# GpSimd's queue issues 112 weight transfers that SP's queue issued: the second MoE's output weights, and its combined input weights

## The chip, the cores and the metric

The kernel runs on one core of one Trainium2 chip. The time is that of one launch in device microseconds; where several runs of a kernel are shown, the median counts. The engines are TensorE (PE in the profile, its weight loads PEld), VectorE (DVE), ScalarE (ACT), GpSimd (POOL) and SyncE (SP, which here does nothing but issue DMAs).

## The reference, cut to what matters

```python
# attention: 4 batches, 8 heads, 576 positions, head_dim 64
q_rot, k_rot = rotate(q), rotate(k)                  # rotary embedding
scores = np.matmul(q_rot, k_rot.transpose(0, 1, 3, 2)) / np.sqrt(64)
attn = softmax(scores)
x = np.matmul(attn, v)                               # -> [2304, 512]
# first MoE: 512 -> 768 -> 512
h = np.maximum(np.maximum(x @ w1, x @ w2), x @ w3)
x = h @ moe_w_out
# second MoE: 512 -> 2048 -> 512
h = x @ moe2_w_in
g = h * (1.0 / (1.0 + np.exp(-h)))
out = g @ moe2_w_out
```

Some weights come as words of 8 bytes; the kernel makes fp32 values of them ("narrows" them) on the chip.

## The kernel before

**Stages.** One fused kernel. From the start to about 545 us it runs attention, tile by tile (a tile is up to 128 query positions of two heads), and between the tiles the first MoE for the batches whose attention is finished; beside both, the weights are prepared. Up to about 620 us the first MoE's last batch follows, and from there on the second MoE. Products of fp32 values are made from high and low fp16 halves, and the second MoE's two layers use seven products in place of eight (as in Strassen's method), for which sums of weight blocks are needed.

**Attention around the change.** For each pair of heads q and k are loaded (`load_qk`, L305 and L308), rotated on GpSimd (`rope_steps`: L366, L367 and L370 for three pieces of the tile, nine steps in all) and transposed on TensorE (`qk_turn`, L387). For each tile TensorE makes the scores (L433 to L443), VectorE their maximum (`tile_max`, L453), ScalarE the exponentials (L460) and their normalisation (`tile_norm`, L472); four DMAs from SP's queue move them between partitions (`tile_move`, L511, pt<-e), VectorE turns blocks of 32x32 in place (`tile_flip`, L533), and TensorE multiplies by v (L578).

**Narrowing.** `narrow_w2` runs 32 pieces of 128x256 for w_in ("wi") and then 32 for w_out ("wo"). A piece is loaded (L858, z64, 256 KB, four buffers), ScalarE takes its high half into z (L229, four buffers), VectorE adds the low half (L241, L248, L249), ScalarE measures it (L155), and the narrowed piece is stored in DRAM: L833 for wi (zwi), L838 for wo (zwo). A z buffer comes round again four pieces later.

**Combined items.** When wi is narrowed and its scale is known, `prep_w8` makes 16 items. Item k loads four blocks from zwi (L965, za, 256 KB, two buffers); GpSimd makes four sums of them (L971, zs, two buffers); ScalarE casts the blocks to fp16 high halves (L948) and VectorE makes the low halves (L952), in w8o (three buffers), for the four loaded blocks and for the four sums; each half is stored in DRAM (L979, w8scr, 256 KB). The second MoE reads w8scr (`w8_load`, L1376 and L1379) and zwo (`prep_w7`, L1001) from about 545 us on.

**What sets the order.** The engines run in order, each its own list. The lists come from a scheduler that simulates the program as it is written (`TileContext` with `schedule_with_timeline_sim=True`), within data dependences, the rings of buffers, and marks (`tc.issue_after`) that keep an instruction behind another one. The load L858 stands behind such a mark: `last["load"]`, the latest load of q and k. All DMAs are issued by SP, but for a few by ScalarE at the start.

Of the kernel before, what the change touches and what calls it, by code (L numbers as in the profile page):

```python
# [22 lines left out]
def fused_kernel(  # L23
# [22 lines left out]
    nc = tc.nc  # L46
# [62 lines left out]
    w8scr = dram.tile([P, NF2 // 2, 2, 2, 8, P], F16, name="w8scr")  # L109
    zscr = {nm: dram.tile([P, KC * (F2 // 512) * 512], F32, name="z" + nm) for nm in ("wi", "wo")}  # L110
# [56 lines left out]
    def flat(t):  # L167
        return t.rearrange("p a b -> p (a b)")
# [112 lines left out]
    last = {}  # L281
# [538 lines left out]
    def narrow_w2(W, src, nm):  # L820

        part = {}
        M = W.m * 512 // 256
        for n in range(M + 5):
            if n >= 5:
                W.measure(n - 5)
                if nm == "wi":
                    i, o = divmod(n - 5, 2)  # L830
                    q, c = divmod(i, KC)
                    half, f = divmod(4 * q + 2 * o, HB)
                    nc.sync.dma_start(  # L833
                        out=zscr[nm].rearrange("p (f c a i n) -> p f c a i n", c=2, a=2, i=2, n=P)[:, f:f + 2, c % 2, c // 2, half],
                        in_=W.t[n - 5].rearrange("p (f n) -> p f n", n=P),
                    )
                else:
                    nc.sync.dma_start(out=zscr[nm][:, (n - 5) * 256:(n - 4) * 256], in_=W.t[n - 5])  # L838
            if 3 <= n <= M + 2:
                with tc.issue_after(last["max"]):  # L840
                    W.narrow_low(part.get(n - 3))
                    W.narrow_b(n - 3, part.pop(n - 3, None))
            if 2 <= n <= M + 1:
                if wide:
                    W.t[n - 2] = z_p.tile([P, 256], F32, tag="z", name="z")
                with tc.issue_after(exps[-1]):
                    W.narrow_a(n - 2, part.get(n - 2), low=False)
            if n < M:
                i, o = divmod(n * 256, 512)
                if nm == "wi":  # L850
                    q, c = divmod(i, KC)
                    from_ = src[c * P:(c + 1) * P, q * 512 + o:q * 512 + o + 256]
                else:
                    from_ = src[i * P:(i + 1) * P, o:o + 256]
                if wide:
                    part[n] = z64_p.tile([P, 256], w1.dtype, tag="z64", name="z64")
                    with tc.issue_after(last["load"]):
                        nc.sync.dma_start(out=part[n], in_=from_)  # L858
                else:
                    W.t[n] = z_p.tile([P, 256], F32, tag="z", name="z")  # L860
                    nc.sync.dma_start(out=W.t[n], in_=from_)
            yield
        t = W.scale_a(n=M)
        yield
        with tc.issue_after(last["score"]):
            W.scale_b("s" + nm, t)
        yield
# [59 lines left out]
    def timed(steps):  # L927

        n = 0
        for t, fn in sorted(steps, key=lambda x: x[0]):  # L930
            while n < t:
                n += 1
                yield
            fn()

    def half_of(W, nm):

        x = const.tile([P, 1], F32, name=nm + "half")
        nc.vector.tensor_scalar(out=x, in0=W.s, scalar1=0.5, scalar2=None, op0=ALU.mult)
        return x  # L940
# [5 lines left out]
    def cast_high(h, x, s, behind):  # L946
        with tc.issue_after(behind):
            nc.scalar.activation(out=h, in_=x, func=AF.Copy, scale=s)  # L948

    def cast_low(l, h, x, s, behind):  # L950
        with tc.issue_after(behind):
            nc.vector.scalar_tensor_tensor(out=l, in0=x, scalar=s, in1=h, op0=ALU.mult, op1=ALU.subtract)  # L952

    def prep_w8(step):

        sw = half_of(WI, "wi")
        steps = []

        def item(k):
            f, c = divmod(k, 2)  # L960
            z, w = {}, {}

            def load():
                z[0] = za_p.tile([P, 4, P], F32, tag="za", name="za")
                nc.sync.dma_start(out=flat(z[0]), in_=zscr["wi"][:, (2 * f + c) * 512:(2 * f + c + 1) * 512])  # L965

            def sums():
                z[4] = zs_p.tile([P, 4, P], F32, tag="zs", name="zs")
                block = lambda i: z[i // 4 * 4][:, i % 4]
                for o, x, y, op in SUMS:  # L970
                    nc.gpsimd.tensor_tensor(out=block(o), in0=block(x), in1=block(y), op=op)  # L971

            def high(a):
                w[a] = w8o_p[0].tile([P, 2, 4, P], F16, tag="w8o", name="w8o")
                cast_high(flat(w[a][:, 0]), flat(z[a]), sw, exps[-1])

            def low(a):
                cast_low(flat(w[a][:, 1]), flat(w[a][:, 0]), flat(z[a]), sw, last["max"])
                nc.sync.dma_start(out=w8scr[:, f, c, :, a:a + 4], in_=w[a])  # L979

            t = k * step
            for d, fn in ((0, load), (2, sums), (2.1, lambda: high(0)), (2.9, lambda: low(0)), (3, lambda: high(4)), (3.9, lambda: low(4))):
                steps.append((t + d, fn))

        for k in range(2 * HB):
            item(k)
        yield from timed(steps)
# [338 lines left out]
    def narrow_all():  # L1326
        yield from narrow_w2(WI, wi2, "wi")
        yield from narrow_w2(WO, wo2, "wo")
# [117 lines left out]
```

## Time and profile before

| | |
|---|---|
| median of 3 runs | 968.02 us (966.81 to 968.2) |
| the profiled execution, its own time | 970.68 us |
| its span | 969.0 us |
| TensorE's mean granted clock | 0.983 |
| TensorE busy | 901.6 us (93%) |
| VectorE busy | 709.6 us (73%) |
| ScalarE busy | 609.4 us (63%) |
| GpSimd busy | 441.1 us (46%) |

The span is the time from the first to the last instruction in the profiled execution; its own time has some 1.7 us around it. Busy shares are means over stages that differ: where an engine is not the one that ends the waits of a stage, its idle time costs nothing. The chain of waits is followed from the last instruction back, at each step to what released it.

### The profile page before, as it was taken

How to read it: one execution, taken by the hardware profiler on the slowest of the kernel's cores; microseconds unless marked ns; L12 is line 12 of the kernel's file. 1: busy time of each engine (PE TensorE's matmuls, PEld its weight loads, DVE VectorE, ACT ScalarE, POOL GpSimd, SP SyncE). 2: the span in 40 equal slices, each digit the busy share in tenths (PEclk: the TensorE clock that was granted, in tenths of full speed). 3: DMA queues.
4: the chain of work that ended last, by engine and by line, in shares of the span. 5: the costliest groups of instructions: out<-in, count | busy, mean ns of one | idle time of the engine just before them, and what ended most of it. 6: DMA issues, size and time to landing. Idle time of an engine off the chain costs nothing.

```text
span 969.0 us, 19018 instructions
## 1 busy us (share of the span) xinstructions
PE 901.6 (93%) x6802; PEld 669.0 (69%) x6802; DVE 709.6 (73%) x1271; ACT 609.4 (63%) x1405; POOL 441.1 (46%) x482
## 2 busy tenths in 40 slices
PE   3887998999999999989998999999998999999997
PEld 1443665666665666656654687788887888888886
DVE  6779888877788676898887677465786766856654
ACT  1987677757788777789877534363654545545442
POOL 6745485870325502321211047264486467464363
PEclk9799998999999999999999999999999999999999
DMA  6953035858888985899999763273543434424101
GB/s 154 285 146 108 14 100 126 186 110 179 200 172 196 221 159 135 218 241 228 263 223 204 183 206 110 63 230 113 157 158 99 136 122 136 127 87 137 61 1 44
DMA packets 178798, 146.29 MB, mean 151 GB/s; under 512 B 50960, under 2 KB 160272, under 8 KB 178704
## 3 DMA queue, kind: packets, MB, share of 16 engines
q1 hardware_dynamic: 177200, 144.36, 58.0%
q8 instruction: 54, 0.88, 0.4%
q10 hardware_dynamic: 1504, 0.72, 0.3%
q14 instruction: 40, 0.33, 0.1%
HBM read 90.51 MB, written 26.21 MB: 120 GB/s over the span
## 4 chain that ended last, share of the span: by engine, by line
PE 54%; DMA 8%; DVE 8%; ACT 5%; POOL 4%; issue 3%; SPq 3%; DVEq 0%; ACTq 0%; POOLq 0%
PE m L673 12%; PE m L1103 7%; DMA pt<-e 5%; PE mb L1103 5%; PE c L1166 4%; PE b L1166 4%; PE a L1166 3%; PE xp L578 3%; PE s L443 3%; PE mg L673 3%; POOL gsum L1050 2%; PE d L1166 2%; SPq L511 2%; DVE pt L533 1%; DVE nb L453 1%
## 5 line engine op out<-in xcount | busy, mean ns | idle before, releaser
L673 PEld LDWEIGHTS <-w 128*128 128x128 f16 x1632 | 159.1, 98 | 61.0 <-issue 17.8
L673 PE MATMUL m<-x,w 128*128 128x256 f16 (+1 forms) x1356 | 186.9, 286 | 10.6 <-DVE t L692 5.4
L1166 PEld LDWEIGHTS <-g 128*128 128x128 f16 x1485 | 145.8, 98 | 17.2
L1103 PEld LDWEIGHTS <-w8s 128*128 128x128 f16 x1344 | 131.2, 98 | 16.3 <-issue 1.0
L453 DVE TENSOR_REDUCE nb<-s 128x2 f32<-128x1152 f32 (+1 forms) x80 | 98.6, 1233 | 40.7 <-PE s L443 34.1
L460 ACT ACTIVATE e<-s,nb 128x576 f32<-128x576 f32 x144 | 105.3, 736 | 29.8 <-DVE nb L453 27.2
L472 ACT ACTIVATE e<-e,rec 128x576 f32<-128x576 f32 x144 | 104.1, 767 | 9.3 <-DVE rec L470 8.9
L366 POOL TENSOR_TENSOR w<-qk,sin_sb 128x512 f32<-128x512 f32 (+2 forms) x40 | 43.4, 1087 | 128.1 <-DMA qk<-in_q_dram 122.5
L443 PE MATMUL s<-T 64*128 64x512 f32 x256 | 80.7, 701 | 0.0
L578 PE MATMUL xp<-pt,vd 128*64 128x256 f32 (+1 forms) x512 | 76.5, 414 | 0.2 <-DVE pt L533 0.2
L533 DVE STREAM_TRANSPOSE pt<-pt 128x1024 f32<-128x1024 f32 (+1 forms) x60 | 67.7, 1129 | 11.9 <-DMA pt<-e 11.6
L971 POOL TENSOR_TENSOR zs<-za 128x128 f32<-128x128 f32 x32 | 17.1, 554 | 119.9 <-DVE w8o L952 46.1
L1117 POOL TENSOR_TENSOR z<-t 128x256 f32<-128x256 f32 x32 | 27.1, 847 | 89.0 <-DVE t L1109 53.9
L1055 DVE SCALAR_TENSOR_TENSOR g<-gsum,sg,g 128x1024 f16<-128x1024 f32 x36 | 49.2, 1372 | 24.5 <-ACT g L1054 24.1
L1054 ACT ACTIVATE g<-gsum,sg 128x1024 f16<-128x1024 f32 x36 | 40.9, 1143 | 37.8 <-POOL gsum L1050 37.8
L673 PE MATMUL m<-h,wo 128*128 128x256 f16 (+1 forms) x448 | 61.7, 286 | 0.0
L673 PEld LDWEIGHTS <-wo 128*128 128x128 f16 x512 | 49.7, 98 | 14.7 <-issue 2.0
L578 PEld LDWEIGHTS xp<-pt,vd 128*64 128x64 f32 x512 | 35.1, 136 | 34.4 <-issue 12.3
L944 POOL TENSOR_TENSOR z<-z 128x256 f32<-128x256 f32 x32 | 30.1, 964 | 42.1 <-DMA z<-zwo 41.6
L1166 PE MATMUL b<-w,g 128*128 128x256 f16 x376 | 48.5, 273 | 0.0
L1166 PE MATMUL c<-w,g 128*128 128x256 f16 x376 | 48.1, 274 | 0.0
L1166 PE MATMUL a<-w,g 128*128 128x256 f16 x376 | 47.9, 273 | 0.0
(266 smaller groups left out, 1998.1 us busy)
## 6 DMA issues: line engine op xcount, KB each, us to landing
w8s<-w8scr SPq DMA_DIRECT2D x64, 448.0 KB, 4.3
pt<-e SPq DMA_DIRECT2D x192, 128.0 KB, 4.1
z<-in_moe_w_in_dram SPq DMA_DIRECT2D x32, 256.0 KB, 3.6
z<-in_moe_w_out_dram SPq DMA_DIRECT2D x32, 256.0 KB, 3.9
w8scr<-w8o SPq DMA_DIRECT2D x32, 256.0 KB, 3.6
w<-in_moe_w_dram SPq DMA_DIRECT2D x6, 768.0 KB, 5.0
wo<-in_moe_w_dram SPq DMA_DIRECT2D x6, 768.0 KB, 5.4
qk<-in_q_dram SPq DMA_DIRECT2D x32, 128.0 KB, 3.6
```

The lines of the kernel that those rows point to most:

```text
L366: tt(out=w4, in0=t4, in1=sin2, op=ALU.mult)
L443: last["s"] = last["score"] = nc.tensor.matmul(s[:, o:o + 512], qs[r], kt[r], start=True, stop=True).ins
L453: x = nc.vector.tensor_reduce(out=nb[:, 0:m], in_=both(s, 0, 960, 576) if m > 1 else s[:, 0:576], op=ALU.max, axis=AX.X, negate=True)
L460: x = nc.scalar.activation(out=e[:, HK[g]], in_=s[:, SK[g]], func=AF.Exp, bias=nb[:, g:g + 1], accum_out=sm[:, g:g + 1])
L472: nc.scalar.activation(out=e[:, HK[g]], in_=e[:, HK[g]], func=AF.Copy, scale=r[:, g:g + 1])
L533: nc.vector.transpose(out=x, in_=x)
L578: nc.tensor.matmul(xp[r, 0:n], v4[:, g, c, :], turned(c, g), start=False, stop=(c == 3))
L673: x = nc.tensor.matmul(ps[:, 0:n], l, r, start=(first and i == 0), stop=(not more and i == len(passes) - 1))
L1054: nc.scalar.activation(out=h, in_=x, func=AF.Copy, scale=sg_t[jb])
L1055: nc.vector.scalar_tensor_tensor(out=l, in0=x, scalar=sg_t[jb], in1=h, op0=ALU.mult, op1=ALU.subtract)
L1103: nc.tensor.matmul(o, l, r, start=(i == 0), stop=(i == len(passes) - 1))
L1166: x = nc.tensor.matmul(ps, l, r, start=first, stop=last_, skip_group_check=True)
```

## The change

Four groups of DMAs go from SP's queue (`nc.sync`) to GpSimd's (`nc.gpsimd`): the stores of narrowed pieces of w_out (L838, 32), the loads of w_out's pieces (L858, only where `nm` is "wo", 32), the loads of the items (L965, 16) and the stores of the items' halves (L979, 32). w_out's loads also lose the mark that keeps them behind the latest load of q and k. The loads and stores of w_in's pieces stay on SP, as do all transfers of attention. What is computed, the buffers and their numbers stay the same.

```diff
--- before.py
+++ after.py
@@ -835,7 +835,7 @@
                         in_=W.t[n - 5].rearrange("p (f n) -> p f n", n=P),
                     )
                 else:
-                    nc.sync.dma_start(out=zscr[nm][:, (n - 5) * 256:(n - 4) * 256], in_=W.t[n - 5])
+                    nc.gpsimd.dma_start(out=zscr[nm][:, (n - 5) * 256:(n - 4) * 256], in_=W.t[n - 5])
             if 3 <= n <= M + 2:
                 with tc.issue_after(last["max"]):
                     W.narrow_low(part.get(n - 3))
@@ -854,8 +854,8 @@
                     from_ = src[i * P:(i + 1) * P, o:o + 256]
                 if wide:
                     part[n] = z64_p.tile([P, 256], w1.dtype, tag="z64", name="z64")
-                    with tc.issue_after(last["load"]):
-                        nc.sync.dma_start(out=part[n], in_=from_)
+                    with tc.issue_after(last["load"]) if nm == "wi" else nullcontext():
+                        (nc.sync if nm == "wi" else nc.gpsimd).dma_start(out=part[n], in_=from_)
                 else:
                     W.t[n] = z_p.tile([P, 256], F32, tag="z", name="z")
                     nc.sync.dma_start(out=W.t[n], in_=from_)
@@ -962,7 +962,7 @@
 
             def load():
                 z[0] = za_p.tile([P, 4, P], F32, tag="za", name="za")
-                nc.sync.dma_start(out=flat(z[0]), in_=zscr["wi"][:, (2 * f + c) * 512:(2 * f + c + 1) * 512])
+                nc.gpsimd.dma_start(out=flat(z[0]), in_=zscr["wi"][:, (2 * f + c) * 512:(2 * f + c + 1) * 512])
 
             def sums():
                 z[4] = zs_p.tile([P, 4, P], F32, tag="zs", name="zs")
@@ -976,7 +976,7 @@
 
             def low(a):
                 cast_low(flat(w[a][:, 1]), flat(w[a][:, 0]), flat(z[a]), sw, last["max"])
-                nc.sync.dma_start(out=w8scr[:, f, c, :, a:a + 4], in_=w[a])
+                nc.gpsimd.dma_start(out=w8scr[:, f, c, :, a:a + 4], in_=w[a])
 
             t = k * step
             for d, fn in ((0, load), (2, sums), (2.1, lambda: high(0)), (2.9, lambda: low(0)), (3, lambda: high(4)), (3.9, lambda: low(4))):
```

The lists of the other engines hardly change. On GpSimd, the list has 503 rows in place of 391. The place below lies in the last rope (qk_4464 is the tile of q and k that it turns, w_4816 its scratch, cos_sb and sin_sb the tables), at about 390 us in the trace of before; names with a number are tiles, the number telling one buffer's use from the next.

```order
+L971 TENSOR_TENSOR zs_4679<-zs_4679,za_4489 128x128
+L979 DMA w8scr_136<-w8o_4496 128x2x512
+L965 DMA za_4677<-zwi_137 128x512
+L858 DMA z_3_4675<-in_moe_w_out_dram 128x256
+L838 DMA zwo_138<-z_4485 128x256
 L366 TENSOR_TENSOR w_4816<-qk_4464,sin_sb_120 128x128
+L971 TENSOR_TENSOR zs_4679<-za_4489,zs_4679 128x128
+L979 DMA w8scr_136<-w8o_4581 128x2x512
+L971 TENSOR_TENSOR zs_4847<-za_4677 128x128 x2
+L858 DMA z_0_4723<-in_moe_w_out_dram 128x256
+L838 DMA zwo_138<-z_4575 128x256
```

The rope's step L366 is the only row that stands there in both lists: around it now stand issues of all four groups, and the sums L971 of the items in za_4489 and za_4677, which all stood behind the rope's last step before. In the same way the first two items' loads L965 and sums now stand before and between the steps of an earlier rope (qk_3941, the third from the end).

On SP, the same stretch of the list:

```order
-L858 DMA z_0_4477<-in_moe_w_out_dram 128x256
-L838 DMA zwo_138<-z_4330 128x256
-L979 DMA w8scr_136<-w8o_4417 128x2x512
-L965 DMA za_4489<-zwi_137 128x512
 L717 DMA yscr_135<-t_4602 128x320
 L511 DMA pt_4454<-e_4380 32x8x128 x4
```

The load and the store of a piece, the store of an item's half and the load of an item are gone from the place ahead of the first MoE's store (L717) and of the four DMAs of a tile of attention (L511), which stay in their order.

## Rows read from the trace of the kernel before

**Rows 1.** the page: part 4, shares of the chain; part 5, one group.

```profile
PE 54%; DMA 8%; DVE 8%; ACT 5%; POOL 4%; issue 3%; SPq 3%; DVEq 0%; ACTq 0%; POOLq 0%
L1117 POOL TENSOR_TENSOR z<-t 128x256 f32<-128x256 f32 x32 | 27.1, 847 | 89.0 <-DVE t L1109 53.9
```

**Rows 2.** busy time by engine, 392 to 545 us, columns named first.

```profile
core 0: us, PE busy (x) PEld busy (x) DVE busy (x) ACT busy (x) POOL busy (x), PEclk, DMA share, GB/s
392.00:545.00 153.00, 142.78 (x952) 90.10 (x951) 127.54 (x257) 128.11 (x354) 28.52 (x57) 1.00 0.95 228
```

**Rows 3.** the chain of waits in 392 to 545 us, its shares by line.

```profile
by line: DMA pt<-e 24.7%; PE m L673 11.5%; issue 8.5%; SPq L511 7.3%; ACT e L472 4.8%; DVE nb L453 4.4%; PE xp L578 4.0%; PE s L443 3.5%; DVE pt L533 3.4%; DMA z<-in_moe_w_out_dram 3.0%; ACT e L460 2.8%; ACT junk L155 2.8%; DVE z L249 2.4%;
```

**Rows 4.** the waits in 392 to 545 us: us in total, times, longest.

```profile
DVE pt L533 <- DMA pt<-e: 9.1, 4, 3.5
```

**Rows 5.** SP issues by line, 380 to 560 us: ns min/median/max, first and last.

```profile
L858 SPq DMA_DIRECT2D z<-in_moe_w_out_dram x28: 332/411/1043, 382.6 to 520.7; - x28
L838 SPq DMA_DIRECT2D zwo<-z x32: 319/432/748, 383.0 to 543.4; - x32
DMA to landing us min/median/max: 1.7/3.8/5.5
L965 SPq DMA_DIRECT2D za<-zwi x14: 320/404/483, 384.0 to 525.7; - x14
L979 SPq DMA_DIRECT2D w8scr<-w8o x32: 370/434/1826, 383.6 to 545.0; - x32
```

**Rows 6.** timeline of ScalarE and SP: start us, us, engine, line, operation.

```profile
405.25 1.43 ACT L472 ACTIVATE e<-e,rec 128x576 f32<-128x576 f32 x2
443.96 1.43 ACT L472 ACTIVATE e<-e,rec 128x576 f32<-128x576 f32 x2
406.55 0.75 SPq L838 DMA_DIRECT2D zwo<-z  x1
407.39 2.67 SPq L511 DMA_DIRECT2D pt<-e  x4
445.42 2.64 SPq L511 DMA_DIRECT2D pt<-e  x4
```

**Rows 7.** DMA issues in 392 to 545 us: KB each, median us to landing.

```profile
w8scr<-w8o SPq DMA_DIRECT2D x30, 256.0 KB, 3.7
z<-in_moe_w_out_dram SPq DMA_DIRECT2D x27, 256.0 KB, 3.9
zwo<-z SPq DMA_DIRECT2D x31, 128.0 KB, 3.8
za<-zwi SPq DMA_DIRECT2D x13, 256.0 KB, 4.0
```

**Rows 8.** timeline of GpSimd and VectorE at 304 us.

```profile
304.10 1.44 POOL L370 TENSOR_TENSOR qk<-qk,w 128x512 f32<-128x512 f32 x1
304.36 1.33 DVE L248 TENSOR_SCALAR z<-z 128x256 int32<-128x256 int32 x1
```

**Rows 9.** VectorE groups, 392 to 545 us: busy us, mean ns, idle before.

```profile
L248 DVE TENSOR_SCALAR z<-z 128x256 int32<-128x256 int32 x29 | 9.9, 340 | 0.0
L249 DVE SCALAR_TENSOR_TENSOR z<-z,z 128x256 int32<-128x256 int32 x31 | 14.1, 456 | 0.1
```

**Rows 10.** timeline of GpSimd, last rope and first sums behind it.

```profile
381.62 1.80 POOL L366 TENSOR_TENSOR w<-qk,sin_sb 128x512 f32<-128x512 f32 x1 [48.49 <-DMA qk<-in_q_dram]
391.30 0.52 POOL L367 TENSOR_TENSOR qk<-qk,cos_sb 128x128 f32<-128x128 f32 x1
391.90 0.71 POOL L370 TENSOR_TENSOR qk<-qk,w 128x128 f32<-128x128 f32 x1
394.11 0.46 POOL L971 TENSOR_TENSOR zs<-za,zs 128x128 f32<-128x128 f32 x1
```

**Rows 11.** timeline of ScalarE at 412 us.

```profile
412.55 0.76 ACT L229 ACTIVATE z<-z 128x256 f32<-128x256 f32 x2
```

**Rows 12.** transposes of the last rope result, 420 to 445 us.

```profile
L387 PE MATMUL tr<-ident,qk x8: 272/272/331, 429.5 to 437.6; 128*128 128x128 f32 x8
```

## The prediction

> **What bounds the kernel now.** I read the chain that ended last first [rows 1]: TensorE's work is 54% of it, and DMA and VectorE have 8% each. The transfer to look at there is pt<-e (exponentials moved for the attention's turn). The moved instructions live between the last rope and the end of attention, so I then read busy time in 392 to 545 us alone [rows 2]: of 153 us TensorE works 142.8, VectorE 127.5, ScalarE 128.1, the DMA engines 95%, and GpSimd 28.5. So TensorE has some 10 us of idle time there, VectorE and ScalarE are five sixths full and in order, and DMA is nearly full. What comes late on VectorE or ScalarE has little room to hide. The chain within that stretch [rows 3] says which transfer ends waits: pt<-e holds 24.7% of it, SP's issuing of pt<-e another 7.3%, and of the moved transfers only the loads of w_out appear, with 3.0%. The waits view [rows 4] has the other side: VectorE's flip L533 waited 9.1 us for pt<-e.
>
> **What the change removes.** SP loses 32 loads L858, 32 stores L838, 16 loads L965 and 32 stores L979: 112 issues at medians of 0.41, 0.43, 0.40 and 0.43 us [rows 5], some 48 us of SP. Is SP late? At 445.42 it issues pt<-e, whose producer L472 (started 443.96, 1.43 us) ended at 445.39: 0.03 us, although a burst of moved issues stood ahead. At 407.39 it issues pt<-e behind a store begun at 406.55, and the producer L472 (405.25 and 1.43) had ended at 406.68: 0.7 us late [rows 6]. So the issue time freed is worth something between 0 and 0.7 us for one flip. The transfers themselves stay the same: 101 of the 112 fall into this stretch (30 + 27 + 31 + 13), at 128 or 256 KB [rows 7]. With the DMA engines at 95%, bytes that leave SP's queue still pass the same engines. The gain that remains is that pt<-e may no longer stand behind them in SP's queue. Bounds: 0, and the 9.1 us that L533 waits. I take 2 us, nearer to the lower end, because the engines and not the queue are what is full.
>
> **What it adds: issues on GpSimd.** No row of before shows a DMA issued by GpSimd, so its cost c must be bounded. From below: 0.41 us, what SP takes. From above: 1.44 us, a rope step on GpSimd beside VectorE work [rows 8]. Between: GpSimd takes 847 ns for a sum of 128x256 where VectorE takes 456 ns for an operation of two inputs of that shape [rows 1, 9], 1.9 times; 1.9 x 0.43 = 0.8 for one of the short issues, and 1.9 x 0.62 (a fourth of the 2.64 us for four pt<-e issues, [rows 6]) = 1.2. I take c = 1.1, near the upper of these two, as these transfers are twice or equal in size to pt<-e.
>
> The Trainium skill ("DMA: Bandwidth & Descriptors", Latency and other measured facts) gives a first byte after about 0.6 us on the sync and scalar path and about 1 us on GpSimd's. By that ratio the issue would cost 1.67 x 0.43 = 0.72 us, an estimate from that page, and the sum would come out with no lateness; no row of before shows a GpSimd issue to hold against it.
>
> **First place that decides.** GpSimd runs in order, and the new order puts the moved DMAs between the steps of the last rope (qk_4464) and the sums. Its data come at 381.62, and before the change its eighth step starts at 391.30 [rows 10]: seven steps take 9.68 us. In the new order 16 moved DMAs, from the load into z_0_4477 to the store of z_4575, and six sums of 0.46 us [rows 10] stand with those seven steps. That store is then issued by 381.62 + 9.68 + 2.8 + 16c = 394.1 + 16c, and landed 3.8 us later [rows 5]. ScalarE's second L229 of the pair at 412.55 (0.76 us for both, so it starts at 412.93, [rows 11]) writes that buffer again, and waits for the landing. Break-even is c = (412.93 - 394.1 - 3.8)/16 = 0.94. At 1.1 the store lands at 415.5, 2.6 us late. Behind the waiting L229 on ScalarE stand L948 and the L472 that makes the next pt<-e; so VectorE's flip and TensorE's products wait too, and with 10 us of idle on TensorE in all I count the 2.6 in full.
>
> **The rest of the stretch.** 153 us less 28.5 of own work leave GpSimd 124.5 us for 101 DMAs: 1.23 us each [rows 2, 7]. At c = 1.1 that is 111 us, 91% full with the sums, in an order fixed beforehand in which a DMA that waits for its producer holds up those behind it. Ahead of it lie stores whose buffers come round again after four pieces (L838) or three (L979). Bounds for the sum of these small waits: 0, and one more lateness as large as the first, 2.6; I take 1.5. The rope itself is covered: its transposes L387 start at 429.5 [rows 12], against a rope that ended at 392.6 and would now end near 392.6 + 2.8 + 17.6 + 4 of waits = 417 at c = 1.1 [rows 10]. The loads L965 moved forward to an earlier rope wait only for a store of the same data, and I cost that at nothing, as GpSimd is idle for 48.49 us before 381.62 [rows 10].
>
> **VectorE beside GpSimd.** At 304.36 L248 took 1.33 us beside the rope step of 304.10 on GpSimd, where its mean in this stretch is 0.34 [rows 8, 9]: some VectorE operations wait out a GpSimd operation. If an issue holds VectorE like that, up to 29 L248 x 111/153 = 0.73 of GpSimd's time in issues x half an issue (0.55) = 11.6 us of VectorE time; if it doesn't, 0. Since VectorE has 25.5 us of idle in the stretch I take 1 on the path.
>
> **Sum.** +2.6 +1.5 +1 -2 = +3.1 us. The profiled execution took 970.68 (span 969.0), 2.7 above the median of 968.02 of the runs; terms are differences read in it, put on the median: 971 us.
>
> **Rivals.** *GpSimd keeps up.* If c is below 0.94 no store is late, the lateness terms vanish, and pt<-e gains: from 2 to the 9.1 us that L533 waits, less 1 for VectorE. Middle: 968 - 4 = 964. For it: the 0.8 from a short SP issue, and that GpSimd is three quarters idle. Against: DMA stays 95% full, so pt<-e may land no sooner.
>
> *GpSimd saturates* Above c = 1.23 every tenth costs 101 x 0.1 = 10 us, because GpSimd's queue then sets the pace of narrowing: stores late, buffers late, ScalarE's L229 late. At 1.44: 21 us beyond a lateness that is by then some 3 us: near 991. It begins to decide at c = 1.23. For it: VectorE is 83% busy in this stretch, and L248's 1.33 us show that the two engines can hold each other up [rows 2, 8]. Against: a DMA issue moves no tile through GpSimd, so it may hold the port for less than a rope step does.
>
> The Trainium skill ("SBUF — State Buffer", SBUF: two separate sides) speaks against this change: GpSimd cannot write descriptors while VectorE runs an operation that takes both shared ports, and a DMA of 620 ns took 3100 ns beside such one. The trace agrees in kind only (1.33 in place of 0.34 us for L248 beside GpSimd); no row of before has the DMA. By it c lies above mine.
>
> *Nothing on the path moves.* SP is not late, moved transfers have slack, bytes are the same: 968. For it: 0.03 us at 445.42; against: 91% fill at c = 1.1.
>
> **How the numbers follow.** Forecast (c of 0.95 to 1.23, +1 to +7): 0.36, of it 0.25 slower by over 0.2% and 0.11 within. Keeps up: 0.32, of it 0.26 faster and 0.06 within. Saturates: 0.22, all slower. Nothing moves: 0.10, of it 0.06 within and 0.02 to each side. 0.2%, 1.9 us, is about what a measurement can tell here. Faster 0.28, same 0.23, slower 0.49. With both signs this likely the range must reach into both: 962 (keeps up, with most but not all of pt<-e's wait gone) to 989 (saturated at c of 1.4 or so); beyond it I leave 0.10 below and 0.09 above. The likeliest case's own range is 969 to 975.
>
> **What would show it.** In the profile after: the duration of GpSimd's DMA issues (my c, the number on which all rests); a wait of ScalarE's L229 for a store zwo<-z near 413 us, 2 to 3 us; GpSimd's queue near full in 392 to 545; the wait of L533 for pt<-e below 9.1 us if the queue mattered; L248's mean above 0.34 us if issues hold VectorE. I am wrong if issues take under 0.9 us, or if descriptors are written off GpSimd's own time, so that it shows them in no row; and, the other way, if they take over 1.3.

## The result, and the profile after

| | before | after |
|---|---|---|
| median | 968.11 us (966.81 to 969.47, 4 runs) | 974.29 us (972.71 to 976.08, 4 runs) |
| ratio, 95% interval | | 1.0066 (1.0051 to 1.0082) |
| profiled execution, span | 970.68, 969.0 us | 976.08, 974.3 us |

The change costs 6.2 us. Measured again in a later job (12 runs against 35 of before), the ratio is 1.0046 (1.0028 to 1.0064): 972.89 against 968.73 us. So it is slower, by some 4 to 6 us. Executions of one kernel spread over up to 9 us here, so a single profile is one draw: the profile after is the slowest of its four runs.

The page of the changed kernel: busy times, the two queues that matter, and the chain's shares.

```profile
PE 902.8 (93%) x6802; PEld 668.5 (69%) x6802; DVE 713.1 (73%) x1271; ACT 608.8 (62%) x1405; POOL 507.3 (52%) x594
q1 hardware_dynamic: 156976, 119.19, 48.1%
q0 software_dynamic: 7936, 25.17, 8.5%
PE 56%; DVE 9%; DMA 8%; ACT 5%; issue 3%; POOL 2%; SPq 2%; DVEq 0%; ACTq 0%; POOLq 0%
```

The moved bytes now go through a queue of their own (q0). Against [rows 1] TensorE's share of the chain is 56%, not 54%, and SP's 2%, not 3%. Busy time in 392 to 545 us, columns as in [rows 2]:

```profile
392.00:545.00 153.00, 142.38 (x932) 89.11 (x929) 128.84 (x254) 126.27 (x350) 91.75 (x160) 0.99 0.89 228
```

GpSimd works 91.75 us in place of 28.52. That is 60% of the stretch, where the prediction reckoned with 91%. Its groups of DMA issues between 380 and 560 us (busy us, mean ns of one, then idle time before them):

```profile
L979 POOL DMA_DIRECT2D w8scr<-w8o x32 | 23.4, 731 | 53.3 <-ACT z L229 14.8 <-ACT rec L469 8.0 <-ACT w8o L948 7.8
L838 POOL DMA_DIRECT2D zwo<-z x32 | 17.9, 559 | 4.3 <-DVE z L249 4.2
L858 POOL DMA_DIRECT2D z<-in_moe_w_out_dram x28 | 15.9, 567 | 3.2 <-DVE nb L453 3.1
L965 POOL DMA_DIRECT2D za<-zwi x14 | 8.2, 589 | 0.0
```

This is the number on which the prediction rested: an issue takes GpSimd 0.56 to 0.73 us, 65.4 us for 106 of them, 0.62 us on average. I had taken 1.1, with a break-even at 0.94. The longest of all (934 ns, a load L965) stayed under it.

**Where the time went.** I followed the same TensorE instruction through both traces. Past 300 us its delay grows in two steps of some 3.0 and 2.4 us, and changes little elsewhere (by 1 us at most, but for a passing 2 us at 510 us that is made good at once); early in the program it wanders by up to 2 us either way, as it does between any two executions.

*First place, 312 to 322 us.* TensorE before and then after (start, us, operation; in brackets the idle time before it):

```profile
316.63 1.79 PE L673 MATMUL m<-x,w 128*128 128x320 f16 x12 [0.93 <-ACT t L690]
318.35 1.95 PE L578 MATMUL xp<-pt,vd 128*64 128x256 f32 x16
```

```profile
318.63 3.20 PE L673 MATMUL m<-x,w 128*128 128x320 f16 x12 [2.55 <-ACT t L690]
321.76 1.51 PE L578 MATMUL xp<-pt,vd 128*64 128x256 f32 x12
```

From one start to the next took 1.72 us and takes 3.13, and the idle time ahead is 2.55 us, not 0.93. The instruction waits for ScalarE's L690, which is late since VectorE was late. VectorE's L241 of that moment, before and after:

```profile
312.36 0.41 DVE L241 TENSOR_SCALAR z<-z 128x256 uint16<-128x256 uint16 x1
```

```profile
312.73 1.37 DVE L241 TENSOR_SCALAR z<-z 128x256 uint16<-128x256 uint16 x1
```

And GpSimd at that time, after the change:

```profile
311.69 0.87 POOL L971 TENSOR_TENSOR zs<-za 128x128 f32<-128x128 f32 x2 [1.11 <-DMA za<-zwi]
312.51 1.27 POOL L370 TENSOR_TENSOR qk<-qk,w 128x512 f32<-128x512 f32 x1
```

L241 starts 0.2 us into the rope step L370 and ends 0.3 us after it: 1.37 us for work of 0.41. Before the change the rope of qk_3941 ended at 311.33, and GpSimd was idle then. What moved it is the two loads L965 ahead of and inside this rope, with the sums behind them; GpSimd also waits 1.11 us for one of the loads to land. L241 makes 1.0 of the 1.6 us by which the idle time grows; the rest comes from shorter hold-ups of VectorE beside GpSimd's next steps (L248, L249, L241 and L249 up to 316.7: together 0.8 us more than before).

With the idle time TensorE's clock fell (at 318.10, shortly before the row of 318.63 begins). The stretches of the changed kernel with the lower clock at this place and at the second one (columns as in [rows 2]):

```profile
318.10:321.50 3.40, 2.87 (x11) 1.58 (x11) 3.40 (x5) 2.33 (x8) 2.65 (x2) 0.50 1.00 188
396.60:400.00 3.40, 3.40 (x15) 1.96 (x13) 3.37 (x5) 3.40 (x10) 3.38 (x6) 0.50 0.59 178
```

A granted clock of 0.50 is the lower level, 1.2 GHz, for 3.4 us each; before, both stretches ran at 1.00.

*Second place, 388 to 400 us.* TensorE's transposes L387 of one tile, before and after:

```profile
391.31 0.63 PE L387 MATMUL tr<-ident,qk 128*128 128x128 f32 x4 [1.25 <-POOL w L366]
394.62 0.60 PE L387 MATMUL tr<-ident,qk 128*128 128x128 f32 x4
```

```profile
395.47 0.63 PE L387 MATMUL tr<-ident,qk 128*128 128x128 f32 x4 [2.01 <-DVE pt L483]
400.46 0.60 PE L387 MATMUL tr<-ident,qk 128*128 128x128 f32 x4
```

Idle time ahead 2.01 in place of 1.25 us, and 4.99 us from the first four to the next in place of 3.31, in the second slow-clock stretch. VectorE just before, in the kernel before and after:

```profile
388.06 1.07 DVE L241 TENSOR_SCALAR z<-z 128x256 uint16<-128x256 uint16 x1
388.93 0.32 DVE L248 TENSOR_SCALAR z<-z 128x256 int32<-128x256 int32 x1
389.17 1.74 DVE L952 SCALAR_TENSOR_TENSOR w8o<-zs,wihalf,w8o 128x512 f16<-128x512 f32 x1
```

```profile
391.95 1.38 DVE L248 TENSOR_SCALAR z<-z 128x256 int32<-128x256 int32 x1
393.25 1.82 DVE L952 SCALAR_TENSOR_TENSOR w8o<-zs,wihalf,w8o 128x512 f16<-128x512 f32 x1
```

Before, L241 and L952 were held up; after, L248 and L952 one behind the other (and L241 at 391.46 a little, 0.69 us). From L241's start to L952's end it is 2.9 us before and 3.6 after, and the difference is TensorE's longer idle time. GpSimd after the change, in the last rope:

```profile
391.91 1.27 POOL L366 TENSOR_TENSOR w<-qk,sin_sb 128x512 f32<-128x512 f32 x1
393.26 1.26 POOL L367 TENSOR_TENSOR qk<-qk,cos_sb 128x512 f32<-128x512 f32 x1
...
413.93 0.46 POOL L370 TENSOR_TENSOR qk<-qk,w 128x128 f32<-128x128 f32 x1
```

L248 waits out the step of 391.91, L952 the step of 393.26. The rope, which took 381.62 to 392.61 before [rows 10], takes 384.98 to 414.39 with the moved issues and sums between its steps: its nine steps meet VectorE's work over 29 us, not 11.

Over 300 to 400 us VectorE's 13 L241 together take 10.4 us, against 7.3 before.

**What holds VectorE.** Sorted over the whole trace after by what GpSimd did meanwhile, L248 (128x256) took 0.32 us on average in 37 cases beside nothing, 0.32 in 10 cases beside a DMA issue, and 0.75 (up to 1.38) in 15 cases beside a tensor operation. L249 (128x256) took 0.41 beside nothing, 0.41 beside an issue, and 0.74 beside a tensor operation. So it is GpSimd's tensor operations that hold VectorE up, and not its DMA issues. Not every operation of VectorE is held: L453 and L533 take no longer beside a tensor operation than alone.

### The profile page after: what moved, and what is told of

Its sections match the earlier page's. It is cut to its first block, busy times and chain, and to the rows that moved or that the text cites. A ratio compares the mean times of both kernels' runs of the same rounds, so it can differ in the third digit from the quotient of the medians.

```text
span 974.3 us, 19061 instructions
## 1 busy us (share of the span) xinstructions
PE 902.8 (93%) x6802; PEld 668.5 (69%) x6802; DVE 713.1 (73%) x1271; ACT 608.8 (62%) x1405; POOL 507.3 (52%) x594
## 4 chain that ended last, share of the span: by engine, by line
PE 56%; DVE 9%; DMA 8%; ACT 5%; issue 3%; POOL 2%; SPq 2%; DVEq 0%; ACTq 0%; POOLq 0%
PE m L673 12%; PE m L1103 8%; PE mb L1103 6%; PE c L1166 4%; PE a L1166 4%; PE b L1166 4%; PE xp L578 3%; PE s L443 3%; PE mg L673 3%; DMA pt<-e 3%; PE d L1166 2%; POOL gsum L1050 1%; DVE nb L453 1%; DMA w8s<-w8scr 1%; ACT e L460 1%
## 5 line engine op out<-in xcount | busy, mean ns | idle before, releaser
L453 DVE TENSOR_REDUCE nb<-s 128x2 f32<-128x1152 f32 (+1 forms) x80 | 98.5, 1232 | 39.8 <-PE s L443 33.5
L366 POOL TENSOR_TENSOR w<-qk,sin_sb 128x512 f32<-128x512 f32 (+2 forms) x40 | 43.0, 1076 | 115.5 <-DMA qk<-in_q_dram 101.9
L443 PE MATMUL s<-T 64*128 64x512 f32 x256 | 77.9, 678 | 0.0
L533 DVE STREAM_TRANSPOSE pt<-pt 128x1024 f32<-128x1024 f32 (+1 forms) x60 | 67.6, 1128 | 11.4 <-DMA pt<-e 11.4
L979 POOL DMA_DIRECT2D w8scr<-w8o x32 | 23.4, 731 | 53.3 <-ACT z L229 14.8
L367 POOL TENSOR_TENSOR qk<-qk,cos_sb 128x512 f32<-128x512 f32 (+2 forms) x44 | 46.5, 1061 | 2.8
```

The lines of the kernel that those rows point to most:

```text
L366: tt(out=w4, in0=t4, in1=sin2, op=ALU.mult)
L367: tt(out=t4, in0=t4, in1=cos2, op=ALU.mult)
L443: last["s"] = last["score"] = nc.tensor.matmul(s[:, o:o + 512], qs[r], kt[r], start=True, stop=True).ins
L453: x = nc.vector.tensor_reduce(out=nb[:, 0:m], in_=both(s, 0, 960, 576) if m > 1 else s[:, 0:576], op=ALU.max, axis=AX.X, negate=True)
L533: nc.vector.transpose(out=x, in_=x)
```

## The experiments

Each is timed against the kernel before on the same chip, 12 runs where not said otherwise. The ratio, with its 95% interval, is not the quotient of the two medians and can differ from it by 0.1%. In the edits "..." marks what is left out.

**1. Two loads alone.**

```diff
-                nc.sync.dma_start(out=flat(z[0]), ...
+                (nc.gpsimd if k < 2 else nc.sync).dma_start(out=flat(z[0]), ...
```

> The kernel before, with only the loads L965 of the first two items on GpSimd's queue (2 of the 112 moved DMAs). On GpSimd the sums of these items then stand before and between the steps of the rope of qk_3941, as in the changed kernel; the lists of TensorE, VectorE and ScalarE are those of the kernel before. Theory 1 (displaced rope): the loss comes from GpSimd's own tensor operations, which now run later and beside VectorE's narrowing at about 312 us (L241 took 1.37 us there after the change, 0.41 before); in the traces of before and after TensorE falls back by 3.0 us between 315 and 322 us, of it some 1.4 in a stretch of 3.4 us at 1.2 GHz behind an idle time of 2.55 us. It expects +2.5 to +3.5 us, 970.5 to 971.6, and L241 near 312.7 us at 1.3 us or more. Theory 2 (each issue on GpSimd costs something, evenly): 2 of 112 of 6.2 us, so 0.1 us: 968.2.

Measured: 970.31 against 968.73, ratio 1.0016 (1.0000 to 1.0032). Its TensorE and VectorE at the first place:

```profile
318.51 3.20 PE L673 MATMUL m<-x,w 128*128 128x320 f16 x12 [2.58 <-ACT t L690]
321.64 1.73 PE L578 MATMUL xp<-pt,vd 128*64 128x256 f32 x14
```

```profile
312.52 1.45 DVE L241 TENSOR_SCALAR z<-z 128x256 uint16<-128x256 uint16 x1
```

The whole picture of the changed kernel is there with 2 of 112 DMAs: L241 at 1.45 us, TensorE idle for 2.58 us, 3.13 us to the next row. The median gives half of the expected 3 us, and its interval reaches zero; the profiled execution (972.83) is the second slowest of the 12. That the 3 us of a profile don't come in every execution fits this, and experiment 4 shows such a case.

**2. The other 110.**

```diff
-                nc.gpsimd.dma_start(out=flat(z[0]), ...
+                (nc.sync if k < 2 else nc.gpsimd).dma_start(out=flat(z[0]), ...
```

> The changed kernel, with the loads L965 of the first two items back on SP's queue (110 of the 112 DMAs moved); GpSimd's list up to the last rope is that of the kernel before. Theory 1 (displaced rope) expects the loss at 315 to 322 us to be gone: 6.2 - 3 = +3.2 us, 971.3, what is left of it at the last rope (388 to 400 us), where DMA issues still stand between the rope's steps. Theory 2 (each issue costs evenly): 110 of 112 of 6.2 us: +6.1, 974.2.

Measured: 972.39, ratio 1.0035 (1.0017 to 1.0053). The first place is clean (one row of TensorE, idle time 0.65 us):

```profile
316.82 1.79 PE L673 MATMUL m<-x,w 128*128 128x320 f16 x12 [0.65 <-ACT t L690]
```

1.6 and 3.7 us are together 5.3, a little over what the whole change cost in the same job (4.2 in medians, 4.5 by the ratio). Within these intervals the two parts make up the whole.

**3. All that lies behind the last rope.** The first nine loads and five stores of w_out, the first four items' loads and first two items' stores go back to SP (w_out's nine loads with their mark):

```diff
+ L838: (nc.sync if n < 10 else nc.gpsimd).dma_start(...
+ L858: (nc.sync if nm == "wi" or n < 9 else nc.gpsimd).dma_start(...
+ L965: (nc.sync if k < 4 else nc.gpsimd).dma_start(...
+ L979: (nc.sync if k < 2 else nc.gpsimd).dma_start(...
```

> The changed kernel, with those DMAs back on SP's queue that stand before or inside the last rope on GpSimd's list: the first four items' loads, the first two items' stores, w_out's first nine loads and first five stores. 90 DMAs stay on GpSimd, all behind the last rope, and GpSimd's tensor operations stand in the order of the kernel before. Theory 1 (displaced rope) expects almost all of the loss to be gone: 968 +-1. Theory 2 (each issue costs evenly): 90 of 112 of 6.2 us: +5.0, 973.1. A gain (under 966) would mean that a freed queue of SP is worth something by itself.

Measured: 968.95, ratio 1.0005 (0.9988 to 1.0022). 90 of 112 DMAs show no cost and no gain clear of noise. An even price per issue (3.6 us of the 4.5 for 90 of 112) is out, since the interval ends at 2.1 us, and so is a gain from a relieved SP of more than 1.2 us.

**4. The changed kernel again.**

> The changed kernel again, for a second profile. Theory 1 expects VectorE's L241 near 312.7 us (trace time) long again, at 1.3 us or more, and TensorE some 3 us behind the kernel before after 322 us, and near 974 us in all. A third theory (chance): the stretches of 3.4 us at 1.2 GHz at 318 and 397 us are chance; then they lie elsewhere or nowhere in this trace, and the delay that TensorE picks up there is some 1.5 us smaller at each place.

Measured: 972.89, ratio 1.0046 (1.0028 to 1.0064). In this trace the same instruction at the first place came after 1.33 us of idle time:

```profile
316.42 1.79 PE L673 MATMUL m<-x,w 128*128 128x320 f16 x12 [1.33 <-ACT t L690]
```

GpSimd ran the same list, but some 0.85 us earlier against VectorE: L241 met only the end of the step L370 and took 0.53 us, and no stretch of slow clock followed there. TensorE lost 0.8 us at this place and 0.5 at the second one. So theory 1's long L241 and its 3 us did not come again: the collision is in the order, and how much it costs changes from execution to execution. The third theory is half right: the slow stretches are not in every execution, the idle time ahead of them is.

**5. The sums without a DMA.**

```diff
+ sums = lambda n, c: [nc.gpsimd.tensor_tensor(out=o[0][:, 0], in0=flat(t[:, c:c + 2, :]), ...
+ sums(4, 0)                          # ahead of the rope of qk_3941
+ ...; sums(2 * (i == 1), lo)         # behind L367 and L370 of its second part
```

> The kernel before with no DMA moved, and eight more sums of 128x128 on GpSimd (results unused) between the steps of the rope of qk_3941: about the tensor work that the first two items' sums put there in the changed kernel. All lists but GpSimd's are those of the kernel before. Theory 1 (displaced rope: GpSimd's tensor operations hold up VectorE's) expects about what the two moved loads cost in the first experiment, +1.6 us (0 to 3): 970.3, with L241 or L248 of VectorE stretched to over 1 us near 312 us in the trace. The rival, that a DMA issued by GpSimd is itself the cost (its issue, its descriptors, its transfer), expects 0: 968.7.

Measured: 968.31 against 968.83, ratio 1.0007 (0.9990 to 1.0023). Its profile has the idle time of the first place, without any DMA on GpSimd:

```profile
316.12 1.79 PE L673 MATMUL m<-x,w 128*128 128x320 f16 x12 [1.67 <-ACT t L690]
```

1.67 us in place of 0.93; the clock did not fall behind it. The stretched L241 or L248 that theory 1 expected is not in this trace (the longest there is 0.70 us); the stall adds up from shorter hold-ups. The median, and the ratio, are no different from no change, as the rival had it, nor is the ratio clearly different from the 1.0016 of the first experiment. So displaced tensor work alone does make a stall; that it makes the first experiment's cost is not shown.

**6 and 7. Rope steps of half the length.** In the changed kernel and in the kernel before:

```diff
-                return rope_steps(t, w, nc.gpsimd, ((0, 8), (8, 16), (16, 18)))
+                return rope_steps(t, w, nc.gpsimd, ((0, 4), (4, 8), (8, 12), (12, 16), (16, 18)))
```

> The changed kernel with each 128x512 step of the ropes of batches 1 to 3 cut into two of 128x256 (some 0.65 us each in place of 1.3; 72 more GpSimd instructions). Theory 1 expects the longest hold-up of a VectorE operation to halve, so that the distance to the same cut in the kernel before (next run) shrinks from 4.5 us to 2.2. If the cost lies in the DMA issues or in what waits for the transfers, the distance stays at 4 to 5 us.

> The kernel before with the same cut of the rope's steps, as the base for the run above. Theory 1 expects a small gain by itself, since the ropes of the kernel before hold up VectorE too (L248 took 1.33 us at 304 us): 967 (966 to 969). If steps of any length cost the same, 968.7, or a little more for 72 further instructions.

Measured: 967.96, ratio 0.9998 (0.9986 to 1.0010), and 964.69, ratio 0.9960 (0.9947 to 0.9973), against 968.83. The distance is 3.3 us, between the 2.2 and the 4 to 5 that were to tell the theories apart, so it decides nothing. In the profile of 6 the stall at the first place is still there (2.26 us of idle time, and the slow stretch), so shorter steps did not remove it. But the cut by itself gains 4.1 us: this version beats both kernels.

Part of that gain can be seen in the traces. At 262 to 268 us in the kernel before, VectorE's L241, L699 and L241 take 1.51, 1.47 and 1.15 us beside steps of 1.27 to 1.46 us of a rope, and TensorE sits idle for 0.83 and 0.64 us; in 7 the three take 0.44, 0.41 and 0.61 us, both idle times are gone, and TensorE gains 1.9 us on the kernel before (1.8 in 6). At the second place 7 gains another 0.9 us.

```profile
262.73 1.51 DVE L241 TENSOR_SCALAR z<-z 128x256 uint16<-128x256 uint16 x1
```

```profile
263.20 0.44 DVE L241 TENSOR_SCALAR z<-z 128x256 uint16<-128x256 uint16 x1
```

**8, 9 and 10. Which early DMAs cost at the last rope.** Experiment 3 with, in addition, the items' six (8), w_out's nine loads and five stores (9), or w_out's nine loads alone (10):

```diff
 8   L965: (nc.sync if k < 2 else nc.gpsimd)...   L979: nc.gpsimd...
 9   L858: (nc.sync if nm == "wi" else nc.gpsimd)...   L838: nc.gpsimd...
10   L858: (nc.sync if nm == "wi" else nc.gpsimd)...
```

> The third experiment's kernel (90 DMAs on GpSimd, all behind the last rope; 968.95 us), and in addition the early DMAs of the items: the stores of the first two items' halves and the loads of the third and fourth (6 DMAs), which stand inside the last rope; the sums of the third item stand between its steps as well. w_out's first nine loads and first five stores stay on SP. Theory 1 (work between the rope's steps displaces the rope against VectorE) expects a good part of the 2.9 us between the second and the third experiment: +1 to +3 over 968.95, about 970.9. The rival, that w_out's early loads and stores, late behind rope steps, make that difference, expects 0: 969.

> The third experiment's kernel (90 DMAs on GpSimd behind the last rope), and in addition w_out's first nine loads and first five stores on GpSimd (14 DMAs before, in and just behind the last rope); the early DMAs of the items stay on SP. The kernel with both groups early on GpSimd (all but two items' loads) had a ratio of 1.0035, the one with the items' group alone 1.0002. If the cost at the last rope lies in w_out's early pieces, this run has about 1.003: 971.7. If it takes both groups together (the rope is then drawn out furthest, from 11 to some 20 us), or if that ratio was a chance high, it has about 1.0005: 969.3.

> The third experiment's kernel and in addition w_out's first nine loads alone on GpSimd (four of them ahead of the last rope, one inside it, four behind); all early stores stay on SP. If early loads cost because they start at another time (they lose the mark that held them behind the loads of q and k), this run costs as the run above, 1.003. If stores inside the rope are what costs, or nothing does, 1.0005: 969.3.

Measured: 968.32 against 968.83, ratio 1.0002 (0.9987 to 1.0017); 968.50 against 967.60, ratio 1.0005 (0.9992 to 1.0018); 969.09 against 967.60, ratio 1.0022 (1.0007 to 1.0038). Neither of the two groups in 8 and 9 alone costs what both together do, and theory 1's +1 to +3 us for 8 did not come: work between the steps of the last rope is not enough by itself. TensorE's row at the second place in 8 and in 9, against 1.25 us before:

```profile
389.67 0.63 PE L387 MATMUL tr<-ident,qk 128*128 128x128 f32 x4 [1.02 <-DVE pt L483]
```

```profile
389.23 0.63 PE L387 MATMUL tr<-ident,qk 128*128 128x128 f32 x4 [0.92 <-DVE pt L483]
```

The ropes of 8 and 9 take some 14 and 18 us, that of experiment 2 takes 28. Experiment 10 is a part of 9 and measured higher; with these intervals the two don't differ clearly, and I draw nothing from it.

**11. The 110 again.**

> The second experiment's kernel again (110 DMAs on GpSimd, all but the first two items' loads), whose profile showed no loss where its median did: 0.5 us at the last rope. If its ratio of 1.0035 was real, 972 again, with a loss at the last rope in the trace of the second profile; if it was chance, near 969.

Measured (11 runs): 971.72 against 967.60, ratio 1.0046 (1.0030 to 1.0062). The cost is real, and this profile has it at the second place:

```profile
389.42 0.63 PE L387 MATMUL tr<-ident,qk 128*128 128x128 f32 x4 [2.00 <-DVE pt L483]
394.41 0.60 PE L387 MATMUL tr<-ident,qk 128*128 128x128 f32 x4
```

2.00 us of idle time, and 4.99 us to the next four, in place of 3.31, as in the changed kernel. In the first profile of this kernel the idle time is there and the slow clock is not, and the place cost 0.5 us:

```profile
391.97 0.63 PE L387 MATMUL tr<-ident,qk 128*128 128x128 f32 x4 [1.72 <-DVE pt L483]
```

Both profiles of the 110 lose time at a third place as well, near 530 us, where no rope runs. VectorE and TensorE there, in the profile of experiment 2:

```profile
530.06 1.25 DVE L533 STREAM_TRANSPOSE pt<-pt 128x1024 f32<-128x1024 f32 x1 [3.58 <-DMA pt<-e]
532.20 0.43 PE L673 MATMUL m<-h,wo1f 128*128 128x320 f16 x2 [2.16 <-DVE t L692]
```

L533 waits 3.58 us for the transfer pt<-e (3.45 in experiment 11, 1.91 before, 1.73 after), and TensorE's row behind it comes after 2.16 us of idle time (2.03; 0.49 before; 0.32 after). In experiment 2 the clock falls there too, at 533.3, and TensorE loses some 3 us and makes good 1.1 of them by 552 us; in experiment 11 it loses 1.5. So a part of the 110's cost in these traces is a later transfer of attention and no displaced rope. The profiles after and of experiment 4 lose at most 0.6 us there, so it is not shown that it comes regularly.

**12. Steps of a quarter.**

```diff
-                return rope_steps(t, w, nc.gpsimd, ((0, 8), (8, 16), (16, 18)))
+                return rope_steps(t, w, nc.gpsimd, [(i, i + 2) for i in range(0, 18, 2)])
```

> The kernel before with each 128x512 step of the ropes of batches 1 to 3 cut into four of 128x128 (0.46 to 0.5 us each). The cut into two gained 4.0 us (ratio 0.9960). If what a VectorE operation waits is the rest of one GpSimd step, a quarter gains a little more than a half: another 0.5 to 2 us, less some for GpSimd's longer ropes (27 instructions in place of 9, some 13 us in place of 9.7): 963 to 965. If the gain came from the other order that the cut brings, not from the length, 968 or any other time.

Measured (7 runs): 970.70 against 967.60, ratio 1.0034 (1.0020 to 1.0047). Slower, where the half gained: the length of one step is not the whole of it. The ropes take 27 instructions here, and with either cut the lists of TensorE and VectorE change by some ten rows. The trace shows a place: between 160 and 180 us TensorE falls back by 9 us against the kernel before, of which it makes good 4 by 280 us. It waits there for GpSimd, which prepares the first MoE's weights (L175) only behind rope steps that run without a pause up to 165.4 us, and the clock is at 0.50 for 10.2 us, before for 6.8:

```profile
166.22 1.03 PE L673 MATMUL m<-h,wo1f 128*128 128x256 f16 x4 [4.12 <-POOL wo1f L175]
```

## Why the prediction was right or wrong

The time (971, range 962 to 989) and the sign came out; the reasons, step by step, mostly did not. That the sum came near was luck: none of its four terms came as it was taken, and what made most of the loss that the traces show had been costed at nothing.

- **The cost c of an issue** was mis-sized: 1.1 us taken, 0.62 measured, between the 0.41 that was the lower bound and the 0.8 worked out from a short SP issue. The estimate from the Trainium skill ("DMA: Bandwidth & Descriptors", Latency and other measured facts), 0.72, was nearer than mine. The moved loads and the stores of w_out's pieces also land later, which is the direction of that page's longer first byte: zwo 4.7 us after its issue, 3.8 before [rows 7]. But pt<-e, still on SP, lands 0.7 us later too, so the first byte is not shown to be the reason.
- **The first late store** (+2.6) did not happen. No row has L229 waiting for a DMA. The store of z_4575 and the L229 in question, GpSimd and then ScalarE:

```profile
412.55 0.54 POOL L838 DMA_DIRECT2D zwo<-z  x1
```

```profile
417.96 0.75 ACT L229 ACTIVATE z<-z 128x256 f32<-128x256 f32 x2
```

The store landed 3.4 us after its issue, at 415.9, and the second L229 of the pair starts at 418.29: 2.4 us to spare. The issue was late, though not for the reason given: with c = 0.62 the sum 394.1 + 16c, moved by the 3.4 us that the rope starts later, would be 407.4. The other 5 us are waits of the in-order queue for its producers, which my calculation left out.
- **The later waits** (+1.5) rested on a queue 91% full; it was 60% full, and experiment 3 shows 90 issues without a measurable cost. The profile after has no wait for one of these stores; those of experiments 2 and 11 have one each, of ScalarE's L948 for a store L979, 0.7 and 0.8 us.
- **The gain on pt<-e** (-2) is not there. Issues in 392 to 545 us with KB and median us to landing, after, and pt<-e before:

```profile
pt<-e SPq DMA_DIRECT2D x74, 128.0 KB, 4.8
w8scr<-w8o POOLq DMA_DIRECT2D x28, 256.0 KB, 3.9
zwo<-z POOLq DMA_DIRECT2D x30, 128.0 KB, 4.7
za<-zwi POOLq DMA_DIRECT2D x13, 256.0 KB, 5.0
```

```profile
pt<-e SPq DMA_DIRECT2D x76, 128.0 KB, 4.1
```

VectorE's wait for it between 380 and 560 us, after and before:

```profile
DVE pt L533 <- DMA pt<-e: 11.4, 7, 3.1
```

```profile
DVE pt L533 <- DMA pt<-e: 11.6, 6, 3.5
```

In 392 to 545 us alone it is 6.6 us against the 9.1 of [rows 4], but only since a wait of 2.14 us now ends at 545.08, just outside. Out of SP's queue, the moved transfers still share the engines with pt<-e, which lands 0.7 us later. This was the doubt named beside the term, and it should have taken the term to zero.
- **VectorE beside GpSimd** (+1) names the two engines that do collide, but the wrong partner. Not issues hold VectorE (L248 beside an issue alone took 0.32 us, as beside nothing); GpSimd's tensor steps do (0.75), which the issues push to other places. L248's mean in 392 to 545 us did rise as the prediction's sign had it, from 0.34 to 0.375 us, for that other reason. The row was in hand [rows 8], and the order showed which steps moved. Read like that, the term would have been the first one.
- **Costed at nothing: the two loads moved into an earlier rope.** This step failed outright. I asked whether the loads were late and whether GpSimd was free, and not what GpSimd's displaced steps would then stand beside. Two of 112 DMAs made 3 us of loss in two profiles (after, and the first experiment), and 1.6 us in the median.
- **The rivals.** "Keeps up" had its condition fulfilled (c under 0.94) and the time still rose, since the gain on pt<-e was not there and the displaced steps cost. "Saturates" fell with c. The trap that the Trainium skill describes for it ("SBUF — State Buffer", SBUF: two separate sides), an issue of 620 ns stretched to 3100 beside VectorE, shows here only in small. Of the 80 issues of loads and of w_out's stores eight met an L248 of VectorE; six of them took 0.63 to 0.93 us, while 70 of the other 72 took 0.54 to 0.58. The longest ends 0.1 us after the L248 that starts inside it:

```profile
425.19 0.93 POOL L965 DMA_DIRECT2D za<-zwi  x1
```

```profile
425.70 0.31 DVE L248 TENSOR_SCALAR z<-z 128x256 int32<-128x256 int32 x1
```

What the same section says of tensor operations, that one of the two engines holds the shared ports for its whole instruction and the other waits, agrees with the trace: L241 took 1.37 us for 0.41 beside a step of 1.27.

**What stays open.** The medians say +1.6 for the two loads and +3.4 to +4.5 for the other 110. The two places show 0.5 to 0.8 us of delay each without a slow-clock stretch, and 2.4 to 3.1 us with one; that agrees with the medians only if such a stretch follows in many executions. Four traces of the changed kernel, its parts or its cut form have one (after, experiments 1, 6 and 11) and two have none (2 and 4), which is too few to count. That VectorE is held by GpSimd's tensor steps is shown row by row; that this makes the whole cost in time is not: the sums without a DMA (experiment 5) and the items' early DMAs (experiment 8) made no cost clear of noise, and the 110 also lose time at 530 us to a late pt<-e. The profiles of experiments 2 and 11 are also faster than their medians, so some of the 110's cost may lie where no profile caught it. Of the half steps' 4 us some 1.3 are not located.

## What to carry to other kernels

Moving DMA issues to an idle compute engine is not free when that engine also has tensor work in the same list: ask first what its own instructions will stand beside once they are pushed back, and only then what an issue costs. Read the order for what moved on the receiving engine, and hold each displaced step against the other engine's rows at its new time. Here the cheap form of the change is to move only the issues behind the engine's last tensor block (experiment 3, no loss clear of noise), and the worthwhile one is another: GpSimd steps of half the length beside VectorE (experiment 7, 4 us). Shorter still is not better: in experiment 12 GpSimd comes late to work that TensorE waits for.

## What the runs showed of the hardware

- A DMA issued by GpSimd occupies it for 0.54 to 0.93 us, 0.73 for the stores of halves; of the loads and w_out's stores, those that met VectorE's L248 were stretched by 0.1 to 0.4 us in six of eight cases (trace after).
- Beside a tensor operation of GpSimd, VectorE's L248 and L249 took 0.75 and 0.74 us on average in place of 0.32 and 0.41; beside a DMA issue of GpSimd they took no longer than alone.
- Moved to GpSimd's queue the same bytes went in larger packets: in 392 to 545 us 34.85 MB moved in both kernels, in 31676 packets after and 42988 before, at a DMA busy share of 0.89 in place of 0.95, without a gain in time.
- At the two places, idle times of TensorE of 2.0 to 2.6 us came with 3.4 us at 1.2 GHz in all five cases (twice after, experiments 1, 6 and 11), and ones of 1.3 to 1.74 us (experiments 2, 4, 5 and 10) in none; so a stall of 0.8 to 1.6 us more cost up to 3 us. It is no rule for other places: in the kernel before, this row of TensorE comes after 2.59 us, and no slow clock followed, while in experiments 1 and 7 the same row, after 2.67 and 2.72 us, has the lower clock beside it and takes 4.99 and 4.93 us.

```profile
513.64 3.42 PE L673 MATMUL m<-x,w 128*128 128x320 f16 x24 [2.59 <-DVE t L692]
```
